# Two-layer MoE behind decayed attention: the first 256 queries' chain leads, score blocks share a bank, the decay's tiles lie on the output buffers

## The chip, the cores and the metric

One core of one Trainium2 chip. The number is the device time of one execution in microseconds (us). TensorE (PE) multiplies matrices from SBUF into PSUM, VectorE (DVE) and ScalarE (ACT) work on both memories, GpSimd (POOL) on SBUF alone, and SyncE (SP) issues nearly all DMAs.

## What is computed

```python
scores = scale * q @ k.T + (cum[:, None] - cum[None, :])      # cum = cumsum(log(clip(f)))
scores = where(causal, scores, -1e9); attn = softmax(scores); x = attn @ v
x = x.reshape(2304, 512)                                      # 4 batches, 8 heads, 576 tokens, 64 a head
h = relu(x @ w_in);  x = (s * h * h + b) @ w_out              # 512 -> 2048 -> 512
h = x @ w_in2;       y = (relu(h) + alpha * min(h, 0)) @ w_out2
```

All inputs are float32, and the result is wanted at that precision: MoE products are made of three passes over values split into a high and a low part.

## The kernel before

All work is written as tasks with an engine (or a choice of engines), a priority from the table `PLAN` and the buffers that they use. A list scheduler in the kernel file runs over them when the program is built and writes the instructions of each engine in the order in which it starts them; on the chip each engine keeps this order and waits on semaphores. Where the scheduler finds PE with nothing to do in the first 50 us of its own reckoning, it puts in a filler (line 482): a matmul of `unit` into the bank `h`, which nobody reads.

The attention of batch 0 is cut into units. Units 0 to 3 are the *pair units*: two heads each and only the first 256 queries, so that blocks 128x128 (chunk 0) and 128x256 (chunk 1) arise for each head. Units 4 to 11 are single heads with the rest of batch 0's queries (128x384, 128x512, and a block for the last 64 rows), later units whole heads of batches 1 to 3. For each block: `t_mm` (line 879, a float32 matmul for batch 0) fills a bank of the ring `s` (three banks), `t_max` (line 887, DVE) adds the mask, writes the block to an `e` tile and takes the row maximum, `t_exp` (892, ACT) takes the exponential and the row sum, `t_eps` (895) and `t_rec` (902) make the reciprocal for a group of blocks, `t_norm` (909, POOL) scales, PE transposes (954), ACT copies to `pt` (963, 965), PE multiplies with `v` (1007), and the output is split into `x` (1013, 1018). A MoE step is line 1057 into `h`, the ReLU (1067, ACT), 1070 to 1080, and line 1089 into `a`.

The decay enters the scores as extra rows of the operands `lk` and `lkx`. For the pair units they are made on chip: `ct` is the running sum of log f (clamp 674, Ln 675, scan 676), copied to the query side (771), multiplied by a column of the selector `sel` on the key side (775), beside a copy of the selector (768, POOL) and ones (765). For other units they go through DRAM: `c8_d` (float32 rows) and, from unit 16 on, `aug_d` (split rows, lines 682 to 689). `ft`, `c8`, `ct`, `aug` and `sel` lie in the pool `fpool`; `to_p1` closes it and opens the pools of `x`, of the MoE buffers and of the outputs `o` in its place, so the first write to `x` (line 1013) waits until the last reader of `fpool` is done.

The weights (`raw`) are loaded as 64-bit words, scaled (520, ACT), put together with three DVE operations (511, 514, 517) and split (534 ACT, 537 POOL).

Of the kernel before, what the change touches and what calls it, by code (L numbers as in the profile page):

```python
# [8 lines left out]
F32 = mybir.dt.float32  # L9
# [41 lines left out]
    t0=-1.0888,  # L51
    ta=0.01,
    tb=9.6508,
    t1=8.6867,
    t2=16.6003,
    t3=15.3984,
    prep=7.7877,
    prepA=43.6581,
    nf=16,
    cp=22.985,  # L60
    ip=-109.7403,
    vp=-33.3287,
    mq=14.5484,
    grp=2,
    grpA=2,
    max=4.2471,
    pv=5.3929,
    f2=-46.0421,
    ap=-14.4232,
    cd=-144.6316,  # L70
    ek=0,
    rw=29.7964,
    ne=20,
    ev='a',
    xh='va',
    gh='va',
    kl='v',
    nr='p',
    cv=(-73.4345, 20.6093, 18.0342, -19.5027, 151.3319, 1.1636, 65.9701, 48.7936, 48.5269, 0.3075, 62.2567, -7.3405, -47.8266, 117.9491, -31.4032, 18.9361),
    blocks=((-14.544, 1.6623), (1.2546, 1.1614), (0.0818, 2.1196), (2.4326, 2.1883), (1.847, 2.8553), (2.9159, 3.0)),  # L80
# [264 lines left out]
def decay_attention_two_moe(ctx: ExitStack, tc: tile.TileContext, qk, qka, v, f, wi1, wo1, wi2, wo2,  # L345
# [39 lines left out]
    def rdma(dst, src):  # L385
# [10 lines left out]
    open_pool("fpool", side="left")  # L396
# [36 lines left out]
        "pt": ring("att", "pt", 2, [P, PTW], F32),  # L433
        "s": ring("psa", "s", 3, [P, 512], F32),
# [7 lines left out]
        "o": ring("p1", "o", 6, [P, 2 * T], F32),  # L442
# [51 lines left out]
    def unpack(key, fc, prio, cv, after=(), view=None, raw=None, at=0.0):  # L494
# [33 lines left out]
    def convert(key, fc, prio, after=()):  # L528
# [9 lines left out]
        task(("act", ac(512, False), t_hi), r=[(K, "v")], w=[(K, "hi")], bufs=[cv, w], prio=prio)  # L538
# [92 lines left out]
    fpool = pools["fpool"][0]  # L631
    LO, HI, BOTH = slice(64, 96), slice(96, 128), slice(64, 128)
    ft = fpool.tile([P, S], F32, name="ft")
    c8_t = fpool.tile([P, 2, 2, S], F32, name="c8")
    c8 = c8_t[LO]
    sel = fpool.tile([P, 2, NHEAD], F32, name="sel")
    one_t = c8_t[BOTH, 0, 1, :]
    ct_t = fpool.tile([P, S], F32, name="ct")
    ct = ct_t[LO]
    aug = fpool.tile([P, 2, 4, S], F32R, name="aug")[LO]  # L640
    augf = aug.bitcast(F32)

# [3 lines left out]
    AUG = [[(k, i) for k in ("chi", "clo", "nchi", "nclo")] + [("aug1", 0), ("aug1", 1)] for i in range(2)]  # L646
# [9 lines left out]
    startup(("sp", 200, lambda: load(ft[LO], f)), w=["f0"])  # L656
    st.append(task(("ad", 200, lambda: aload(ft[HI], f)), w=["f1"], prio=-103.0))
    startup(("dve", 60, lambda: nc.vector.memset(warm, 1.0)), w=["warm"])
    startup(("act", 1400, lambda: nc.scalar.activation(warm, warm, AF.Ln)), r=["warm"], w=["warm"])
    for k, part in (("selA", LO), ("selB", HI)):  # L660
        startup(("sp", 200, lambda part=part: load(sel[part], sel_in)), w=[k])
    startup(("dve", 540, lambda: nc.vector.memset(one_t, 1.0)), w=["one"])
    st.append(task([("dve", 540, lambda: nc.vector.memset(c8[:, 1, 0, :], 1.0)), ("pool", 530, lambda: nc.gpsimd.memset(c8[:, 1, 0, :], 1.0))], w=["one8"], prio=PLAN["ap"]))
    for a in range(2):
        st.append(task(("pool", 1020, lambda a=a: nc.gpsimd.memset(augf[:, a, 1 - a::2, :], 1.0)), w=[("aug1", a)], prio=PLAN["ap"]))
    startup(("pool", 250, const_sums), w=["constsums"])
    for i, (a, z) in enumerate(FPARTS):
        def part(i=i, a=a, z=z, pr=-100.0 if i == 0 else PLAN["f2"]):
            n, fs, cs = z - a, ft[BOTH, a:z], ct[:, a:z]
# [47 lines left out]
    def add_unit(heads, chunks, t0, t1):  # L717
# [13 lines left out]
        units.append(u)  # L731
        return u

    tm = PLAN["t0"]
    for p in range(NPAIR):
        add_unit([2 * p, 2 * p + 1], [0, 1], tm, tm + PLAN["ta"])
        tm += PLAN["ta"]
# [13 lines left out]
    def prep_f32(u):  # L751
# [12 lines left out]
        def t_one():  # L764
            nc.gpsimd.memset(flat(u)[HI, 0, 0:w], 1.0)
# [896 lines left out]
```

## Time and profile before

| | |
|---|---|
| median of 3 runs | 961.25 us (960.94 to 962.83) |
| profiled execution, its own time | 958.43 us |
| its span, first to last instruction | 956.6 us |
| PE busy / DVE / ACT / POOL | 940.1 / 721.9 / 606.4 / 384.8 us |
| mean granted clock of PE | 0.996 of full speed |

Line 482 counts as PE being busy. "Granted clock" 1.00 is 2.4 GHz, 0.50 is 1.2 GHz. A float32 matmul shows as two records in the trace, so "x8" in a row of such matmuls are four. The end of a matmul's record overlaps the next one; the start times are the better measure of the pace.

### The profile page before, as it was taken

To read this page: it belongs to the slowest core of one execution; us is meant where nothing else is said; L and a number is where in the kernel's file an instruction comes from. 1 tells how busy PE (TensorE), PEld (TensorE's weight loads), DVE (VectorE), ACT (ScalarE), POOL (GpSimd) and SP (SyncE) were. 2 spreads that over 40 slices of the span, in tenths; PEclk is the share of its full clock that TensorE was granted. 3 is DMA by queue.
4 is the path that set the end of the run, shared out by engine and by line. 5 is a ranking of instruction groups with operands and counts; after the bars stand their busy time and mean duration, and the time that the engine had idled before them with its cause. 6 is when DMAs were issued, how large, how long until landed. Compare 5 with 4: busy or idle time off the path is not lost.

```text
span 956.6 us, 18667 instructions
## 1 busy us (share of the span) xinstructions
PE 940.1 (98%) x6382; PEld 848.9 (89%) x6382; DVE 721.9 (75%) x1543; ACT 606.4 (63%) x1455; POOL 384.8 (40%) x425
## 2 busy tenths in 40 slices
PE   7899999999999999999999999999999999999998
PEld 6567798899798988988888888899999999999997
DVE  7688877775877656668796896679986869868686
ACT  5688767564767567798676776565654456544552
POOL 5465653451644104478576744124251422513000
PEclk9999999999999999999999999999999999999999
DMA  7674433531544385596869665995698955889566
GB/s 185 190 217 154 159 119 113 174 125 56 174 135 143 101 309 160 154 303 229 319 220 357 237 218 191 338 340 193 186 314 258 319 177 176 252 252 319 164 188 203
DMA packets 99119, 201.44 MB, mean 211 GB/s; under 512 B 10816, under 2 KB 25504, under 8 KB 98352
## 3 DMA queue, kind: packets, MB, share of 16 engines
q1 hardware_dynamic: 98688, 199.78, 64.5%
q8 instruction: 51, 0.84, 0.4%
q10 hardware_dynamic: 336, 0.47, 0.2%
q14 instruction: 44, 0.36, 0.1%
HBM read 146.75 MB, written 50.51 MB: 206 GB/s over the span
## 4 chain that ended last, share of the span: by engine, by line
PE 92%; DVE 5%; DMA 1%; ACT 1%; issue 0%; POOL 0%; SPq 0%; DVEq 0%
PE b L1328 16%; PE h L1057 15%; PE a L1089 9%; PE b L1092 9%; PE a L1390 8%; PE k L1057 6%; PE k L1390 5%; PE h L1390 5%; PE t L1007 5%; PE t L954 4%; PE s L879 4%; PE a L1092 2%; PE s L874 2%; PE s L875 2%; DVE gq L1315 1%; DVE gq L1268 1%
## 5 line engine op out<-in xcount | busy, mean ns | idle before, releaser
L1328 PE MATMUL b<-wp,gj 128*128 128x256 f32 x1368 | 172.4, 278 | 0.8 <-DVE gj L1315 0.7
L1328 PEld LDWEIGHTS b<-wp,gj 128*128 128x128 f32 x1368 | 169.4, 188 | 1.2 <-DVE gj L1315 1.0
L909 POOL TENSOR_SCALAR e<-e,rec 128x128 f32<-128x128 f32 (+4 forms) x144 | 94.1, 665 | 148.0 <-DVE rec L902 45.5
L1057 PE MATMUL h<-x,i 128*128 128x256 f32 (+1 forms) x864 | 146.4, 318 | 0.0
L1057 PEld LDWEIGHTS h<-x,i 128*128 128x128 f32 x864 | 123.9, 188 | 13.6 <-issue 1.2
L1315 DVE TENSOR_TENSOR gj<-gq,gj 128x384 fp32r<-128x384 f32 x152 | 98.9, 660 | 31.6 <-ACT gj L1313 31.0
L1313 ACT CAST gj<-gq 128x384 fp32r<-128x384 f32 x142 | 73.0, 515 | 68.6 <-PE b L1328 64.9
L1268 POOL TENSOR_TENSOR gq<-gq 128x384 f32<-128x384 f32 x33 | 40.0, 1214 | 161.7 <-DVE gq L1430 141.1
L1089 PE MATMUL a<-g,o 128*128 128x256 f32 x768 | 101.4, 281 | 0.0
L1089 PEld LDWEIGHTS a<-g,o 128*128 128x128 f32 x768 | 94.7, 188 | 2.1 <-issue 0.5
L892 ACT ACTIVATE e<-e,ngm 128x128 f32<-128x128 f32 (+4 forms) x144 | 84.1, 586 | 16.0 <-DVE ngm L887 13.8
L1092 PE MATMUL b<-g,o 128*128 128x512 f32 x384 | 93.4, 389 | 0.0
L1092 PEld LDWEIGHTS b<-g,o 128*128 128x128 f32 x384 | 71.8, 188 | 14.5
L887 DVE CUSTOM_DVE_ANT_0 e<-s,mask 128x128 f32<-128x128 f32 (+4 forms) x144 | 67.1, 480 | 20.4 <-PE s L875 8.9
L1111 POOL TENSOR_TENSOR g<-r,g 128x512 fp32r<-128x512 f32 (+1 forms) x42 | 53.5, 1278 | 67.5 <-ACT g L1108 66.2
L1067 ACT ACTIVATE r<-h 128x256 f32<-128x256 f32 (+1 forms) x76 | 34.0, 448 | 52.1 <-PE h L1057 49.9
L954 PE MATMUL t<-ident,e 128*128 128x128 f32 (+1 forms) x400 | 63.9, 275 | 2.7 <-ACT pt L965 1.5
L965 ACT COPY pt<-t 128x256 f32<-128x256 f32 (+2 forms) x128 | 54.3, 451 | 15.0 <-PE t L954 14.6
L1390 PE MATMUL h<-x,wq 128*128 128x384 f32 x288 | 57.6, 335 | 0.0
L511 DVE TENSOR_SCALAR cv<-raw 128x512 int32<-128x512 int32 x48 | 27.6, 576 | 38.2 <-ACT raw L520 33.2
L954 PEld LDWEIGHTS t<-ident,e 128*128 128x128 f32 (+1 forms) x400 | 46.3, 140 | 9.7 <-issue 2.7
L1007 PE MATMUL t<-pt,v 128*64 128x320 f32 (+4 forms) x448 | 52.2, 366 | 0.1
(177 smaller groups left out, 2005.9 us busy)
## 6 DMA issues: line engine op xcount, KB each, us to landing
wp<-w2o_d SPq DMA_DIRECT2D x168, 256.0 KB
wq<-w2i_d SPq DMA_DIRECT2D x112, 256.0 KB
raw<-in_wi_dram SPq DMA_DIRECT2D x29, 512.0 KB
w2o_d<-wq SPq DMA_DIRECT2D x56, 256.0 KB
w2i_d<-wq SPq DMA_DIRECT2D x56, 256.0 KB
raw<-in_wo_dram SPq DMA_DIRECT2D x27, 512.0 KB
rawqk<-in_qk_dram SPq DMA_DIRECT2D x20, 576.0 KB
v<-in_v_dram SPq DMA_DIRECT2D x20, 320.0 KB
```

The source lines that it names most:

```text
L887: nc.vector.tensor_tensor_reduce(e.t[0:rows, k0:k1], st_.t[0:rows, 0:w], mask[0:rows, m0:m0 + w], -0.125 if u.f32 else -1.0, init, ALU.add ...
L892: nc.scalar.activation(x, x, AF.Exp, bias=ng[0:rows, col:col + 1], scale=-1.0, accum_out=sm[0:rows, col:col + 1])
L909: eng.tensor_scalar(x, x, rc[0:rows, col:col + 1], 1.0, ALU.mult, ALU.mult)
L954: nc.tensor.transpose(pp.t[0:kw, i * P:i * P + P], e.t[:, P * kb:P * kb + kw], ident)
L1007: nc.tensor.matmul(o.t[64 * j:64 * j + 64, a - q0:z - q0], vb.t[0:kr, kb, j, :], uu.pt[jj].t[0:kr, kb * PTS + a:kb * PTS + z], start=(i == ...
L1057: nc.tensor.matmul(ps.t[:, 0:w], wv[:, wl, kc, :], x.t[:, kc, xl, x0:x0 + w], start=(n == 0), stop=(n == 3 * KC - 1))
L1089: nc.tensor.matmul(acc[u // 2].t[:, T * (u % 2):T * (u % 2) + T], wo.t[:, wl, u * P:u * P + P], g.t[:, gl, g0:g0 + w], start=(first and i ...
L1092: nc.tensor.matmul(acc[u].t[:, 0:w], wo.t[:, wl, u * P:u * P + P], g.t[:, gl, 0:w], start=(first and i == 0), stop=end)
L1313: task([("act", ac(TH, False), lambda g=g, qv=qv: nc.scalar.copy(g.t[:, 0, :], qv())), ("dvp", dv2(TH), lambda g=g, qv=qv: nc.vector.tenso ...
L1315: task(("dvp", dv(TH), lambda g=g, qv=qv: nc.vector.tensor_tensor(g.t[:, 1, :], qv(), g.t[:, 0, :].bitcast(F32), ALU.subtract)), r=[("G", ...
L1328: nc.tensor.matmul(y[t // 2].t[:, T * (t % 2):T * (t % 2) + T], g.t[:, gl, t * P:t * P + P], wop[k].t[:, wl, :], start=(fresh and k == 0 a ...
L1390: nc.tensor.matmul(b.t[:, 0:TH], wb.t[:, wl, k * P:k * P + P], x[:, k, xl, :], start=(start and m == 0), stop=(m == 5), skip_group_check=True)
```

## The change

The units keep their work. What changes:

- The pair units' priorities (`tA`) now lie ahead of everything else, and the tasks of the startup are ordered for them: both scans directly behind each other, with a broadcast column of ones; all eight `t_q`/`t_k` products before the first maximum; the rows of `c8` on POOL or DVE, `f` loaded before the identity.
- The query side is now the running sum times the selector's column (`t_q`), and the key side's counterpart are ones (`t_one` for both sides), so the copy of the selector on POOL is gone.
- Both blocks of a head go into one bank (`s0`), one `e` tile and one transpose bank; one copy of 384 columns (`transposes_two`) takes them to `pt` or the new ring `pa`. The value product of the pair units goes to the ring `a`. Reciprocals are taken for groups of four blocks (`grp`, `grpA`), normalization may go to POOL or ACT (`nr='pa'`), copies of `pt` to DVE or ACT (`ev='va'`).
- `fpool` is gone. `ct`, `c8` and half of `aug` lie in a tile `F` in the place of the six output buffers `o`, the other half of `aug` in the place of `xs`; `x` has memory of its own from the start.
- All numbers of `PLAN` are new.

```diff
 PLAN = dict(
-    t0=-1.0888,
+    t0=11.8757,
-    grp=2,
-    grpA=2,
+    grp=4,
+    grpA=4,
-    ev='a',
+    ev='va',
-    nr='p',
+    nr='pa',
+    tA=-90.0,
...
-    open_pool("fpool", side="left")
+    open_pool("p1", side="left")
+    open_pool("x0", side="left")
+    open_pool("x1", side="left")
...
+    FW = 72 + 6 * 2 * T
+    F = [pools["p1"][0].tile([P, FW], F32, tag="F", bufs=1, name="F_0")]
+    aug0 = pools["p1"][0].tile([P, 2048], F32R, tag="xs", bufs=1, name="aug0")
+
+    def o_at(n):
+        return F[1][:, 72 + 2 * T * (n % 6):72 + 2 * T * (n % 6) + 2 * T]
...
-        "o": ring("p1", "o", 6, [P, 2 * T], F32),
+        "o": Ring(6, o_at),
...
+    ct_t, big = F[0][:, 0:S], F[0][:, S:S + 8 * (S - QA)]
+    c8 = big[LO, 0:4 * S].rearrange("p (a r s) -> p a r s", a=2, r=2)
+    aug = [x[HI].rearrange("p (a r s) -> p a r s", a=2, r=4) for x in (aug0, big.bitcast(F32R))]
...
-        def t_one():
-            nc.gpsimd.memset(flat(u)[HI, 0, 0:w], 1.0)
-
-        def t_sel():
-            nc.gpsimd.tensor_copy(both(1, LO), sel[LO, 0, n:n + 2].unsqueeze(2).to_broadcast([32, 2, QA]))
-
-        def t_q(copy):
-            copy(both(0, LO), ct_t[LO, 0:QA].unsqueeze(1).to_broadcast([32, 2, QA]))
+        def t_one(eng, side):
+            eng.memset(flat(u)[(HI, LO)[side], side, 0:w], 1.0)
+
+        def t_q(eng):
+            for j in range(2):
+                dst, k = flat(u)[LO, 0, QA * j:QA * j + QA], sel[LO, 0, n + j:n + j + 1]
+                if eng is nc.scalar:
+                    eng.activation(dst, ct_t[LO, 0:QA], AF.Copy, scale=k)
+                else:
+                    eng.tensor_scalar(dst, ct_t[LO, 0:QA], k, None, ALU.mult)
...
-            ps = [R["s"].buf() for _ in parts]
-            e = u.e[j, c] = R[f"e{c + 2 * j if u.two else c}"].buf()
+            s0 = P * c if u.two else 0
+            if u.two and c == 1:
+                e = u.e[j, c] = u.e[j, 0]
+            else:
+                ps = [R["s"].buf() for _ in parts]
+                e = u.e[j, c] = R[f"e{2 + (2 * U + j) % 3 if u.two else c}"].buf()
...
+    def transposes_two(u):
+        U = u.i
+        for j in range(2):
+            u.pt[j] = R["pt" if U % 2 else "pa"].buf()
+            pp, x = R["t"].buf(), u.pt[j]
...
+            def t_ev(copy, x=x, pp=pp):
+                copy(x.t[:, 0:3 * P], pp.t[:, 0:3 * P])
...
     def to_p1():
-        close_pool("fpool")
-        open_pool("p1", side="left", reuse_waits="tile")
...
+        F.append(pools["p1"][0].tile([P, FW], F32, tag="F", bufs=1, name="F_1"))
```

How this moves instructions. In the rows below a line number is that of the kernel they come from (879 before is 906 after, 887 is 914, 775 is 800, 1013 is 1062); numbers behind a name are buffers; in square brackets are the semaphores waited for, DMAHW being a load. On DVE, from the second scan (`ct` or `F`) to the first row maximum (ISA with `mask`), before:

```order
L676 SCALAR_TENSOR_TENSOR ct<-c_132,ct,ft 64x320 [waits Activation_49]
L775 TENSOR_SCALAR lkx_155<-ct,sel 32x256 x2
L511 TENSOR_SCALAR cv_242<-raw_170 128x512 [waits DMAHW6_49,Activation_49]
L682 CAST aug<-ct 32x256
L514 SCALAR_TENSOR_TENSOR cv_242<-raw_170,cv_242 128x512 [waits DVE_49]
L683 TENSOR_TENSOR aug<-ct,aug 32x256 [waits DVE_49]
L517 SCALAR_TENSOR_TENSOR cv_242<-raw_170,cv_242 128x512 [waits DVE_49]
L689 TENSOR_SCALAR aug<-aug 32x256 [waits DVE_49]
L682 CAST aug<-ct 32x320
L775 TENSOR_SCALAR lk_161<-ct,sel 32x256 x2
L683 TENSOR_TENSOR aug<-ct,aug 32x320 [waits DVE_49]
L887 ISA e_0_292,ngm_126<-s_221,mask 128x128 [waits DMAHW7_49,PE_49]
```

and after, from the first scan on:

```order
L697 SCALAR_TENSOR_TENSOR F_94<-ones,F_94 64x256 [waits Activation_49]
L697 SCALAR_TENSOR_TENSOR F_94<-ones,F_94 64x320 [waits DVE_49,Activation_49]
L796 TENSOR_SCALAR lkx_147<-F_94,sel 32x256 [waits DMAHW3_49]
L796 TENSOR_SCALAR lkx_147<-F_94,sel 32x256
L800 TENSOR_SCALAR lkx_147<-F_94,sel 32x256 [waits DMAHW4_49]
L800 TENSOR_SCALAR lkx_147<-F_94,sel 32x256
L800 TENSOR_SCALAR lkx_155<-F_94,sel 32x256 x2
L800 TENSOR_SCALAR lkx_162<-F_94,sel 32x256 x2
L800 TENSOR_SCALAR lk_169<-F_94,sel 32x256 x2
L914 ISA e_0_270,ngm_139<-s_246,mask 128x128 [waits DMAHW6_49,PE_49]
L914 ISA ngm_139 128x1
L914 ISA e_0_270,ngm_139<-s_246,mask 128x256
```

The weight conversion (`cv`) and the split of the decay (`aug`) no longer stand ahead of the first maximum; the eight scalings of the key side (800) and the two of the first unit's query side (796) follow the scans directly.

On PE, the first score blocks behind the first run of fillers, before:

```order
L879 MATMUL s_221<-lkx_140 128x128 [waits DMAHW3_49,DVE_49,Pool_49]
L879 MATMUL s_225<-lkx_140 128x256
L879 MATMUL s_229<-lkx_140 128x128 [waits DVE_49]
L482 LDWEIGHTS unit
L482 MATMUL h_142<-unit 128x256
```

and after:

```order
L906 MATMUL s_246<-lkx_147 128x128 [waits DMAHW2_49,DVE_49,Pool_49]
L906 MATMUL s_246<-lkx_147 128x256
L906 MATMUL s_254<-lkx_147 128x128 [waits DVE_49]
L906 MATMUL s_254<-lkx_147 128x256
L906 MATMUL s_258<-lkx_155 128x128 [waits DVE_49,DMAHW5_49,Activation_49,Pool_49]
L906 MATMUL s_258<-lkx_155 128x256
L500 LDWEIGHTS unit
L500 MATMUL h_149<-unit 128x256
```

Six blocks in three buffers of the ring (s_246, s_254 and s_258) stand ahead of the next filler, where three blocks in three buffers stood.

On DVE, the first writing of `x` and what stands around it, before (DMAHW2 is the store of `aug` to `aug_d`):

```order
L902 RECIPROCAL rec_125<-sums_123 128x2 [waits Activation_49]
L887 ISA e_2_401,ngm_126<-s_366,mask 128x256 [waits DVE_49,PE_49,Pool_49]
L887 ISA ngm_126 128x1
L902 RECIPROCAL rec_124<-sums_122 128x2 [waits DVE_49,Activation_49]
L1013 CAST x_444<-t_413 128x256 [waits DMAHW2_49,PE_49]
L511 TENSOR_SCALAR cv_452<-raw_297 128x512 [waits Activation_49]
```

and after:

```order
L1062 CAST x_401<-a_379 128x256 [waits PE_49]
L929 RECIPROCAL rec_137<-sums_135 128x4 [waits Activation_49]
L1067 TENSOR_TENSOR x_401<-a_379,x_401 128x256 [waits DVE_49]
L980 COPY pt_392<-t_391 128x384 [waits PE_49]
L980 COPY pt_397<-t_396 128x384 [waits PE_49]
```

The cast to `x` waits for PE alone now; copies of 384 columns from the transposes' banks follow it. On PE as a whole, 134 fillers became 94, of which 45 stand ahead of the first score (38 before); the last 2749 matmuls are in the same order.

## Rows read from the trace of the kernel before

**Rows 1.** The page, part 1: busy us (share of span) x instructions.
```profile
PE 940.1 (98%) x6382; PEld 848.9 (89%) x6382; DVE 721.9 (75%) x1543; ACT 606.4 (63%) x1455; POOL 384.8 (40%) x425
```

**Rows 2.** Groups by line, 0 to 48 us: count | busy us, mean ns.
```profile
L482 PE MATMUL h<-unit 128*128 128x256 bf16 x134 | 22.6, 312 | 0.9 <-POOL sums L654 0.9
```

**Rows 3.** The chain that ended last, 0 to 60 us: start us, us, what.
```profile
24.23 4.71 DMA aug_d<-aug
...
40.28 1.12 PE s L879 x8
...
43.20 1.51 PE s L879 x4
44.70 0.80 PE t L1007 x8
...
47.56 0.44 PE t L954 x4
47.99 1.42 PE h L1057 x12
```

**Rows 4.** PE timeline: start, us, line, operation [idle before <- releaser].
```profile
0.88 7.18 PE L482 MATMUL h<-unit 128*128 128x256 bf16 x38 [0.88 <-POOL sums L654]
...
9.43 3.86 PE L482 MATMUL h<-unit 128*128 128x256 bf16 x33
16.92 1.22 PE L879 MATMUL s<-lkx 128*128 128x256 f32 x2 [3.63 <-DVE ngm L887]
...
30.12 0.78 PE L879 MATMUL s<-lk 128*128 128x256 f32 x2 [2.69 <-DVE ngm L887]
```

**Rows 5.** Two microseconds: length, busy us per engine, PEclk (granted clock), DMA.
```profile
18.00:20.00 2.00, 2.00 (x9) 1.57 (x8) 0.85 (x5) 1.86 (x10) 0.00 (x0) 0.50 0.28 71
```

**Rows 6.** DVE's timeline, 0 to 50 us, columns as in rows 4.
```profile
3.58 1.70 DVE L674 TENSOR_SCALAR ft<-ft 64x256 f32<-64x256 f32 x2 [1.41 <-DMA ft<-in_f_dram]
5.21 1.10 DVE L676 TENSOR_TENSOR_SCAN ct<-c,ft 64x256 f32<-64x256 f32 x1
...
9.40 0.88 DVE L676 TENSOR_TENSOR_SCAN ct<-c,ct,ft 64x320 f32<-64x320 f32 x1
10.32 0.82 DVE L775 TENSOR_SCALAR lkx<-ct,sel 32x256 f32<-32x256 f32 x2
...
14.39 1.63 DVE L775 TENSOR_SCALAR lk<-ct,sel 32x256 f32<-32x256 f32 x2
...
16.56 0.29 DVE L887 CUSTOM_DVE_ANT_0 e<-s,mask 128x128 f32<-128x128 f32 x1
...
29.04 0.42 DVE L1013 CAST x<-t 128x256 fp32r<-128x256 f32 x1 [3.98 <-DMA aug_d<-aug]
```

**Rows 7.** POOL's timeline, 0 to 50 us.
```profile
0.96 1.44 POOL L765 MEMSET lkx<- 32x512 f32 x3
...
2.90 2.20 POOL L665 MEMSET aug<- 32x1152 f32 x2
...
14.61 1.26 POOL L537 TENSOR_TENSOR i<-cv,i 128x512 fp32r<-128x512 f32 x1 [3.62 <-ACT i L534]
```

**Rows 8.** ACT's timeline, 0 to 50 us.
```profile
23.52 0.39 ACT L892 ACTIVATE e<-e,ngm 128x128 f32<-128x128 f32 x1
...
23.91 0.49 ACT L892 ACTIVATE e<-e,ngm 128x256 f32<-128x256 f32 x1
```

**Rows 9.** From the first ReLU to the eighth, columns as in rows 5.
```profile
49.40:107.80 58.40, 57.87 (x400) 42.34 (x399) 49.33 (x131) 47.99 (x143) 33.69 (x38) 1.00 0.61 192
```

**Rows 10.** Groups of ACT there: count | busy, mean ns | idle before, releasers.
```profile
L892 ACT ACTIVATE e<-e,ngm 128x512 f32<-128x512 f32 (+4 forms) x25 | 15.9, 638 | 2.3 <-DVE ngm L887 2.3
L965 ACT COPY pt<-t 128x256 f32<-128x256 f32 (+2 forms) x27 | 11.8, 467 | 2.3 <-PE t L954 2.3
L520 ACT ACTIVATE raw<-raw 128x512 f32<-128x512 f32 x11 | 7.7, 697 | 1.1 <-DMA raw<-in_wi_dram 0.7 <-DMA raw<-in_wo_dram 0.4
...
L1074 ACT ACTIVATE g<-r,small 128x256 fp32r<-128x256 f32 x6 | 3.0, 508 | 0.1
```

More of the change, by code (lines that the diff above doesn't have):

```diff
@@ L628, in outs_of @@
             task(("sp", kb_of(P * 2048), lambda i=i: rdma(w2t_d[p // CH][i][:, p % CH], st_.t[:, i])), r=done, w=[("w2t", p, f"t{i + 1}")], bufs=[st_], prio=prio)
-    fpool = pools["fpool"][0]
     LO, HI, BOTH = slice(64, 96), slice(96, 128), slice(64, 128)
[L633 to L641, printed above, removed]
+    ct_t, big = F[0][:, 0:S], F[0][:, S:S + 8 * (S - QA)]
+    c8 = big[LO, 0:4 * S].rearrange("p (a r s) -> p a r s", a=2, r=2)
+    sel = pools["att"][0].tile([P, 2, NHEAD], F32, name="sel")
+    ones = pools["att"][0].tile([P, 1], F32, name="ones")
+    aug = [x[HI].rearrange("p (a r s) -> p a r s", a=2, r=4) for x in (aug0, big.bitcast(F32R))]
+    augf = [x.bitcast(F32) for x in aug]
+    ft = ct_t
     HF32 = max(H, PLAN["nf"] - H // 2)
     FPARTS = ((0, QA), (QA, S))
-    AUG = [[(k, i) for k in ("chi", "clo", "nchi", "nclo")] + [("aug1", 0), ("aug1", 1)] for i in range(2)]
+    AUG = [[(k, i) for k in ("chi", "clo", "nchi", "nclo")] + [("aug1", 0, i), ("aug1", 1, i)] for i in range(2)]
     st = []
@@ L732, in add_unit @@
         return u
[L734 removed]
+    tm = PLAN["tA"]
     for p in range(NPAIR):
@@ L828, in prep @@
         task(("sp", kb_of(P * 8 * w), t_load), r=["attr"], w=[(U, "raw")], bufs=[u.raw], prio=pr)
-        task(("sp", 100 if not u.two else 700, t_rows), r=["augd"], w=[(U, "rows")], bufs=[u.lk], prio=pr)
+        task(("sp", 100 if not u.two else 700, t_rows), r=[("augd", 0), ("augd", 1)], w=[(U, "rows")], bufs=[u.lk], prio=pr)
         task(("pool", pl1(w) - 80, t_khi), r=[(U, "raw")], w=[(U, "khi"), (U, "klo")], bufs=[u.raw, u.ka], prio=pr)
@@ L917, in scores @@
                 if uu.two:
-                    need += [(uu.i, k) for k in ("raw", "one", "sel", "q", "k")]
+                    need += [(uu.i, "raw"), (uu.i, "one", 0), (uu.i, "one", 1), (uu.i, "q"), (uu.i, "k")]
                 elif uu.f32:
@@ L999, in products, with t_pv @@
             xs = {blk: xbuf(blk) for blk, *_ in pieces}
-            o = R["t"].buf()
+            o = R["a" if u.i < PLAN["pa"] else "t"].buf()
             K = (u.i, "o", part)
-            def t_pv(part=part, q0=q0, seq=seq, o=o):
+            def t_pv(part=part, q0=q0, seq=seq, o=o, step=P if u.two else PTS):
                 for i, (kb, a, z) in enumerate(seq):
@@ L1099, in moe_step @@
                      w=[(K, "h")] + ([("open", name, fc)] if kc == 0 else []), bufs=[ps, x, wi], prio=pr1)
-        PG = ["pg2"] if big else ["p1"]
+        PG = ["pg2"] if big else []
         def g_hi():
```

150 lines of the change are left out of this document (85 added, 65 removed).

## The prediction

> **What bounds the kernel now.** The page first: TensorE (PE) is busy for 940.1 of 956.6 us [rows 1], so the time is the sum of what PE has to do plus whatever keeps it from useful work. But a part of that busy time is not work: line 482 issues filler matmuls into a bank nobody reads, 134 of them, all before 48 us [rows 2]. So I read the start next, in the chain of waits and in PE's timeline, and ask how much of the first 47.56 us was useful. 47.56 is where the last filler ends; from there the chain is solid PE work [rows 3].
>
> Useful by then, priced from [rows 3]: the float32 scores of 384 and 512 columns take 1.51 us, 1.69 ns a column, so the 16 score blocks of the first 256 queries (8 heads of 128+256 columns) are 5.2 us; three pairs of 384+512 blocks 4.5; the block of the last 64 rows 1.12; 27 transposes at 0.11 are 3.0; four value products at 0.80 are 3.2. Together 17.0 us. **Dead time is 47.56 - 17.0 = 30.5 us.** It has three faces. PE stood still for 3.63 us before 16.92 and for 2.69 before 30.12 [rows 4]. After the first stand the granted clock was 0.50, that is 1.2 GHz instead of 2.4, for more than 2 us [rows 5], and a similar stretch followed the second. The rest is fillers.
>
> Why it stood shows in VectorE's (DVE) timeline [rows 6]. The first row maximum (16.56) stands behind the selector products, the decay's split and a weight conversion, and until it has read a score bank PE has no fourth bank. And at 29.04 DVE had idled 3.98 us for the store of aug to DRAM (24.23 to 28.94 in [rows 3]): x, which it wants to write, lies on the memory of aug.
>
> **The change, part by part.** The program's tail is untouched: the last 2749 matmuls, 374 ScalarE (ACT), 544 DVE and 84 GpSimd (POOL) instructions stand in the same order. Useful PE work is the same; fillers go from 134 to 94. So I count dead time anew, up to the last filler of the new order.
>
> *Ahead of the first score* stand 45 fillers instead of 38. The 38 ended at 8.06, and 33 dense ones took 3.86 us, 0.117 each [rows 4]: 8.06 + 7 x 0.117 = 8.9. Is the data there? DVE now begins with four memsets of 32x512 (0.48 each on POOL, [rows 7]), so to about 3.2, where the clamps stood at 3.58 before; then the clamps, Ln on ACT and the two scans, 1.10 and 0.88 [rows 6]: clamps 3.3 to 3.9, first scan 4.5 to 5.6, second to 6.4. The scans read a broadcast column of ones instead of a 64x576 tile; no row shows the form, and I price it as before. Then ten scalings of 32x256. [rows 6] show 0.41 (two in 0.82) and 0.82 (two in 1.63, while POOL ran the two-input subtraction of 14.61 in [rows 7]). I take 0.41, because POOL has one-input work at this place, scalings and memsets. Four make the first unit's operands: 8.05, before PE comes. All ten end at 10.5; by 0.82 at 14.6. Up to 0.5 each they cost PE nothing, by the next paragraph. POOL's selector copies go; ACT scales the other three units' queries meanwhile, six from about 6.5 on, each 0.4 to 0.5 like the exponentials of 128 and 256 columns [rows 8], hidden behind fillers and the first unit's scores.
>
> *Two blocks in one bank.* Three banks now hold six blocks instead of three, so PE runs six before it needs a maximum read. The first maximum of a pair waits for both matmuls: at most the 256-column one, 0.43 us. It costs nothing, as the first three banks are full at 8.9 + 2.0 = 10.9 and DVE comes at 10.5 anyway and is then the slower: 0.29 for 128 columns [rows 6] and at most 0.58 for 256, against PE's 0.65 a pair. PE's eight fillers behind the sixth block last to 11.8. The Trainium skill (PSUM — Partial Sum Buffer, section on bank collisions) speaks against such sharing: no two engines may be in one bank at once. By it each pair is written whole, then read whole, as this order does; the sum stays as it is. With eight evictions less (one of 384 columns for 128 and 256) ACT and DVE save some 1.5 us, used up below.
>
> *The overlay.* x no longer lies on aug: the wait of 3.98 us is gone, with PE's 2.69. The aug store, now in two pieces, still takes about 4.7 us of the queues, and SP issues it ahead of the next two weight loads; what is late next is the scaling of those weights on ACT, at about 30 us.
>
> *The walk.* First maximum 10.5, first exponential 10.9; a pair of exponentials is 0.39 + 0.49 (starts in [rows 8]). Reciprocals now serve four blocks and stand behind twelve maxima: 14.5. POOL and ACT normalize from 14.7, the first transposes are possible at 15.6, when PE has done its 16 scores (8.9 + 0.9 of fillers + 5.2 = 15.0) and five more fillers. From there PE's fillers and ACT run level: ACT's list (16 exponentials 7.0, 6 norms 2.5, reciprocal sums, one eviction and one weight scaling) fills 10.9 to about 22, when PE is at the second value product. I find waits of 0.5 us in all. Useful work up to the last filler is 5.2 + 2.6 + 3.2 + 1.5 + 1.12 + 0.65 = 14.3; the 49 later fillers at 0.11 are 5.4. **Last filler at 8.9 + 5.4 + 14.3 + 0.5 = 29.1, dead time 14.8.** The first MoE step, 5.6 us of work later, ends at 34.8; it ended at 49.41 [rows 3]. **Gain up to here: 30.5 - 14.8 = 15.7 us**, of which 6.3 are the two stands, some 5 the low clock and 4.3 fillers.
>
> *What is given back.* Between the first and the eighth ReLU PE was full before: 57.87 of 58.40 us, ACT at 47.99 [rows 9]. The new order puts more attention in this stretch: 8 score matmuls, 13 transposes and 14 value products more, about 6.8 us, so PE wants 65.2. ACT has 8 more exponentials (0.64 each), 22 norms that POOL used to do, 2 more weight scalings (0.70) and a gate (0.51), 7 evictions less (0.4) [rows 10]. No ACT norm is in the trace; between the gate's 0.51 for 256 columns and the scaling's 0.70 for 512, less their overlap, I take 0.5 (0.4 to 0.7: 8.8 to 15.4). That is 48.0 + 5.1 + 11.0 + 1.4 + 0.5 - 2.8 = 63.2. ACT also waited 3.4 us there for others than PE: 2.3 for maxima, 1.1 for weight loads [rows 10]. 63.2 + 3.4 = 66.6 against 65.2: ACT is the bound by 1.4, and its waits grow when DVE gets some of its evictions. I take 4.5 us, between 0 (ACT ahead) and 12.
>
> **Sum.** 15.7 - 4.5 = 11.2 us off the profiled execution: span 945.4, time 958.43 - 11.2 = 947.2. The three runs' median is 961.25, 2.8 above the profiled execution; the same 11.2 off it gives **950.0 us**.
>
> **Rivals.**
> *A, nothing is given back*: ACT runs ahead of PE, norms nearer 0.4. For it: 0.53 us of PE idleness in that stretch before [rows 9]. Against: ACT at 97% of PE's need. 961.25 - 15.7 = 945.5.
> *B, ACT becomes the bound of the first blocks*: norms at 0.7 and waits doubled make 67.6 + 6.8 = 74.4, nine over PE's 65.2; 954 to 959.
> *C, the start is slow again*: each of the ten scalings waits for POOL, 0.82 us, all done at 14.6. PE has six blocks done and its eight fillers out at 11.8, and stands until 15: as long as the 3.63 us before, and with the half clock after it (some 2 us), 5.5 us lost: 955.5. For it: the 1.63 row, and the clamps, two in 1.70 beside POOL's memset of 2.90 [rows 6, 7]. Against: the scalings of 0.41. The Trainium skill (SBUF — State Buffer, SBUF: two separate sides) has a rule for it: VectorE's two-port modes and GpSimd lock a shared port pair for a whole instruction, and the loser blocks. The two rows agree. By that rule each scaling waits for up to one POOL instruction, which is C.
> *D, slower*: ACT's queue stalls for so long that the head start is spent. Counted by columns as above, the eighth ReLU stands behind 78.0 us of useful work in the new order and 70.4 in the old; at PE's pace of the stretch (58.4 us for 52.5) PE had done as much at about 107.8 + 8.4 = 116 before. The new kernel is slower if ACT gets there later: 34.9 + 63.2 leaves 18 us for waits. The place would be the weight scalings behind the aug store, and the norms behind reciprocals of four blocks. With 22 us it ends at 965. Against: 10.4 us of idleness in all before, most of it for PE.
> *E, the overlay is one tile for six outputs* and could make them wait for each other. The order of the tail shows the same waits as before; under 0.01.
>
> **How the numbers follow.** Forecast (947 to 953) 0.57, A 0.13, B 0.16, C 0.07, D 0.07. The order after 108 us changes too, up to the common tail; of PE's 16.5 us of idleness [rows 1] some 9 lie behind 48 us, and for a sixth of them each end carries 1.5 more. The range 943 to 958 (A less 1.5 and one for the bounds of the scalings and norms; B nearly to its end) leaves out D and little else. 0.2% is 1.9 us, about what a measurement of this kernel can tell from no change: faster 0.88, the same 0.05 (the end of B), slower 0.07.
>
> **What would show it.** 94 fillers, the last ending near 29; no stretch with granted clock 0.50 after the first score; DVE's first maximum near 10.5 and no idle for the aug store ahead of x; the first MoE step ending near 34.8, the eighth ReLU near 104.5; PE idle there of a few us, released by ACT. A first maximum at 14 or later is C, an eighth ReLU past 110 B, past 116 D.

## The result: 951.8 us, a little over the forecast

The changed kernel takes **951.77 us** (median of 4 runs, 950.27 to 952.06) against 961.1 for the kernel before beside it: ratio 0.9897, 95% interval 0.988 to 0.9915. Forecast were 950.0, range 943 to 958, faster with 0.88. Its profiled execution took 952.06 us, with a span of 950.3; that of the kernel before had taken 958.43, 6.4 more.

The page of the changed kernel (engine totals) and its group of fillers, which answer to [rows 1] and [rows 2]:

```profile
PE 934.7 (98%) x6342; PEld 842.7 (89%) x6342; DVE 722.4 (76%) x1558; ACT 622.7 (66%) x1458; POOL 324.2 (34%) x342
...
L500 PE MATMUL h<-unit 128*128 128x256 bf16 x94 | 14.8, 306 | 0.9 <-POOL unit L439 0.9
```

PE's timeline of the changed kernel (columns as in [rows 4]), from the first filler to the end of the first blocks:

```profile
0.88 7.26 PE L500 MATMUL h<-unit 128*128 128x256 bf16 x45 [0.88 <-POOL unit L439]
7.98 2.13 PE L906 MATMUL s<-lkx 128*128 128x128 f32 x12
9.95 1.06 PE L500 MATMUL h<-unit 128*128 128x256 bf16 x8
12.63 2.21 PE L906 MATMUL s<-lkx 128*128 128x128 f32 x12 [1.63 <-DVE ngm L914]
...
30.42 0.51 PE L500 MATMUL h<-unit 128*128 128x256 bf16 x3
37.28 0.91 PE L906 MATMUL s<-lkx 66*128 66x384 f32 x2 [0.52 <-DVE ngm L914]
39.55 0.98 PE L1003 MATMUL t<-ident,e 128*128 128x128 f32 x7 [0.81 <-ACT pt L1014]
...
92.76 0.33 PE L1003 MATMUL t<-ident,e 128*128 128x128 f32 x1 [2.63 <-ACT pt L1014]
```

The two stands of [rows 4], 3.63 and 2.69 us, are gone; one of 1.63 is left, for the first row maximum ("x12" in the rows around it are six score blocks). The last filler ends at 30.93 (47.56 before) and the first ReLU, right behind the first MoE step, starts at 36.79 (49.55 before). Then PE stands again at three places where it hardly did before: 0.52, 0.81 and 2.63 us. DVE's timeline shows why the first maximum, at 11.84, is late:

```profile
3.17 0.53 DVE L695 TENSOR_SCALAR F<-F 64x256 f32<-64x256 f32 x2
4.45 1.67 DVE L697 TENSOR_TENSOR_SCAN F<-ones,F 64x256 f32<-64x256 f32 x2 [0.75 <-ACT F L696]
6.04 0.83 DVE L796 TENSOR_SCALAR lkx<-F,sel 32x256 f32<-32x256 f32 x2
6.91 3.56 DVE L800 TENSOR_SCALAR lkx<-F,sel 32x256 f32<-32x256 f32 x6
10.39 1.42 DVE L800 TENSOR_SCALAR lk<-F,sel 32x256 f32<-32x256 f32 x2
11.84 0.29 DVE L914 CUSTOM_DVE_ANT_0 e<-s,mask 128x128 f32<-128x128 f32 x1
...
19.88 0.43 DVE L1062 CAST x<-a 128x256 fp32r<-128x256 f32 x1
```

The ten scalings take 0.41 (two), 0.59 (six) and 0.71 us (two) each. And the first x, at 19.88, waits for nothing: the 3.98 us behind the store of aug in [rows 6] are gone.

**The clock.** A second record of the same kernel (c_after below) has the same stand of 2.63 us, and yet the granted clock (last but two) differs behind it. Two microseconds at 94, first of the profiled execution of the result, then of that second one, and its stand:

```profile
94.00:96.00 2.00, 2.00 (x12) 1.67 (x12) 1.73 (x7) 1.76 (x7) 0.71 (x1) 0.50 0.25 100
```

```profile
94.00:96.00 2.00, 2.00 (x18) 1.30 (x16) 1.98 (x7) 2.00 (x8) 0.73 (x1) 1.00 0.25 102
```

```profile
92.79 0.33 PE L1003 MATMUL t<-ident,e 128*128 128x128 f32 x1 [2.63 <-ACT pt L1014]
```

The half clock (0.50, that is 1.2 GHz) lasts about 3.5 us and costs half of that; the spans are 950.3 and 948.4. Every run lists its mean granted clock, so an estimate of the loss can be taken out of each: (1 - clock) times the span. The clock is listed to 0.001, so one such value is good to some 0.5 us. The kernel before had 0.992 to 0.997 in the 39 runs that list it, its profiled execution 0.996, so 958.43 - 0.004 x 956.6 = 954.6 at the full clock; those 39 runs come to 954.4 in the mean, and to 954.2, 954.3 and 954.5 on the three chips that ran them. The changed kernel had 0.998 in six of eight runs and 1.000 in two, and those two took 950.27 and 950.22. **So about 4.4 of the 9.3 us between the medians are waits and fillers, and some 5 are a clock that falls less often.** Only the second part moves with the runs: the kernel before had medians of 958.2, 960.0 and 959.9 beside the experiments. Why its clock falls more often is not shown beyond the stands of [rows 4] that are gone.

### The profile page after: what moved, and what is told of

The parts are those of the page before. It is cut to its first block, busy times and chain, and to the rows that moved or that the text cites. A ratio compares the mean times of both kernels' runs of the same rounds, so it can differ in the third digit from the quotient of the medians.

```text
span 950.3 us, 18342 instructions
## 1 busy us (share of the span) xinstructions
PE 934.7 (98%) x6342; PEld 842.7 (89%) x6342; DVE 722.4 (76%) x1558; ACT 622.7 (66%) x1458; POOL 324.2 (34%) x342
## 3 DMA queue, kind: packets, MB, share of 16 engines
q1 hardware_dynamic: 99184, 199.78, 65.2%
## 4 chain that ended last, share of the span: by engine, by line
PE 93%; DVE 4%; ACT 2%; issue 1%; DVEq 0%
PE b L1377 17%; PE h L1106 14%; PE b L1141 9%; PE a L1138 9%; PE a L1439 8%; PE k L1106 6%; PE k L1439 5%; PE h L1439 5%; PE t L1056 5%; PE t L1003 4%; PE s L906 3%; PE a L1141 2%; PE s L901 2%; PE s L902 2%; ACT pt L1014 1%
## 5 line engine op out<-in xcount | busy, mean ns | idle before, releaser
L1141 PEld LDWEIGHTS b<-g,o 128*128 128x128 f32 x384 | 71.8, 188 | 14.6
L936 POOL TENSOR_SCALAR e<-e,rec 128x256 f32<-128x256 f32 (+4 forms) x66 | 42.0, 646 | 105.2 <-DVE rec L927 42.5
L1160 POOL TENSOR_TENSOR g<-r,g 128x512 fp32r<-128x512 f32 (+1 forms) x34 | 45.1, 1329 | 75.5 <-ACT g L1157 71.0
L1003 PE MATMUL t<-ident,e 128*128 128x128 f32 (+1 forms) x376 | 59.3, 277 | 6.2 <-ACT pt L1014 4.2
L1003 PEld LDWEIGHTS t<-ident,e 128*128 128x128 f32 (+1 forms) x376 | 43.6, 140 | 16.6 <-ACT pt L1014 5.7
L1439 PEld LDWEIGHTS h<-x,wq 128*128 128x128 f32 x288 | 49.4, 188 | 0.2
L1056 PE MATMUL t<-pt,v 128*64 128x320 f32 (+3 forms) x416 | 48.3, 368 | 0.2 <-ACT pt L1014 0.2
L1056 PEld LDWEIGHTS t<-pt,v 128*64 128x64 f32 (+1 forms) x416 | 26.0, 135 | 23.6 <-issue 5.1
```

The costliest lines, as they stand in the source:

```text
L1003: nc.tensor.transpose(pp.t[0:kw, i * P:i * P + P], e.t[:, P * kb:P * kb + kw], ident)
L1056: nc.tensor.matmul(o.t[64 * j:64 * j + 64, a - q0:z - q0], vb.t[0:kr, kb, j, :], uu.pt[jj].t[0:kr, kb * step + a:kb * step + z], start=(i ...
L1141: nc.tensor.matmul(acc[u].t[:, 0:w], wo.t[:, wl, u * P:u * P + P], g.t[:, gl, 0:w], start=(first and i == 0), stop=end)
L1160: eng.tensor_tensor(g.t[:, 1, g0:g0 + w], r_of(), g_hi().bitcast(F32), ALU.subtract)
L1439: nc.tensor.matmul(b.t[:, 0:TH], wb.t[:, wl, k * P:k * P + P], x[:, k, xl, :], start=(start and m == 0), stop=(m == 5), skip_group_check=True)
```

## The experiments

Each time is the median of the runs of that kernel; "at 0.998" names the mean granted clock, and "at the full clock, estimated" the mean of the runs less (1 - clock) times the span; for the changed kernel that is 950.1. Most edits that change a task make the planner arrange the whole list anew; where an edit was put in behind the planner, the text says "in the same order".

**c_after: once more, unchanged.** 

> The changed kernel once more, unchanged, as the measure for the other runs beside it. Its ratio to the kernel before was 0.9897 (0.988 to 0.9915); the same is expected here, whatever the level of this chip.

951.84 (950.22 to 952.06), ratio 0.9919 (0.9898 to 0.994). The level of the changed kernel is the same on both occasions; that of the kernel before moves with its clock.

**e1_norms16: ScalarE's normalizations cut to 16 columns, in the same order.**

```
+ if U >= 2 * NPAIR // 2 and U < NPAIR + 2 * H:      # NPAIR <= U
+     x = x[:, 0:16]
  nc.scalar.activation(x, x, AF.Copy, scale=rc[0:rows, col:col + 1])
```

> The changed kernel with the same order of instructions, but ScalarE's normalizations of the units 4 to 19 (one head with all or most of its queries each) scale 16 columns only; the rest of those blocks stays unnormalized. Theory 1 (ACT's work is the bound of the first blocks): ACT is relieved of some 22 x 0.4 = 9 us between the first and the eighth ReLU, PE's idle time there (3.96 us in the changed kernel) falls under 1 us, the stretch of half clock behind the stand at 90 us is gone, and the time is 945 to 948. Rival (PE stood there for banks or weights, not for ACT's load): idle time stays above 3 us and the time within 1 us of the changed kernel's 951.8.

950.35 (949.6 to 952.99). From the first to the eighth ReLU, the stretch of [rows 9], first of c_after, then of this kernel (both at 1.000):

```profile
37.00:106.40 69.40, 65.66 (x453) 47.14 (x454) 58.83 (x169) 63.24 (x174) 29.25 (x27) 1.00 0.60 190
```

```profile
36.80:105.70 68.90, 65.71 (x454) 47.23 (x454) 59.23 (x169) 56.87 (x174) 29.39 (x27) 1.00 0.60 191
```

ACT loses 6.4 us of work and the stretch 0.5; the span goes from 948.4 to 947.8. PE's idle time there is 3.19 us (3.74 in c_after), and the stand at 90 us shrinks from 2.63 to 1.90, as the four normalizations ahead of it in ACT's list are shorter:

```profile
92.07 0.33 PE L1005 MATMUL t<-ident,e 128*128 128x128 f32 x1 [1.90 <-ACT pt L1016]
```

Theory 1 falls: ACT's amount of work is not what bounds these blocks.

**e2_noeps: without the 24 additions of 1e-9, in the same order.**

```
  def t_eps(c0=cols[0], c1=cols[-1] + 1):
-     nc.scalar.activation(sm[:, c0:c1], sm[:, c0:c1], AF.Copy, bias=1e-9)
+     pass
```

> The changed kernel in the same order without the 24 ScalarE instructions that add 1e-9 to the row sums (a sum is at least 1, so float32 keeps it as it is). Each takes 0.2 us alone and about 0.1 between two others. Theory 1 (ACT is the bound between 37 and 108 us): some 1 to 2 us of ACT's work go there, and reciprocals come 0.1 to 0.3 earlier; time 949.5 to 951, PE idle in that stretch 2 to 3.5 us. Rival (ACT's queue is not what PE waits for): 951 to 952.5.

951.73 (950.09 to 953.57); 950.09 at 1.000 against 950.22 for c_after: no difference, which again speaks against ACT as the bound. Its profile shows the half clock at another place, behind the small stands at 37 and 39 us:

```profile
41.00:45.00 4.00, 4.00 (x11) 1.31 (x12) 0.88 (x3) 3.37 (x8) 0.42 (x2) 0.50 0.42 133
```

**e6_evict: the two evictions that PE waits for at 90 us go to VectorE, all else in the same order.**

```
+ if t.idx == 133:                 # last step of a conversion: behind them
+     self.kept = fn
+ elif t.idx in (552, 553):        # the two evictions
+     [o[2] for o in t.opts if o[0] == "dve"][0]()
```

> The changed kernel in the same order but for two evictions of transposes (128x256 each), for which PE stood from 90.14 to 92.76: VectorE does them instead of ScalarE, ahead of the last step of a weight conversion. Theory (PE stood because these evictions are late in ScalarE's list, behind a ReLU, a gate and four normalizations, not because ScalarE has too much to do): the stand shrinks from 2.63 to about 1 us, the half clock behind it is shorter or gone, and the time is 1.5 to 3 us below the changed kernel beside it. Rival (ScalarE or VectorE as a whole is behind): PE stands as long a little later, time within 0.7 us.

The place first. The chain of waits of the changed kernel from 88 us on:

```profile
88.21 0.59 ACT pt L1014
88.80 0.52 ACT o L555
89.31 0.70 ACT e L934 x2
90.01 0.27 ACT r L1116
90.28 1.11 ACT e L934 x2
91.40 0.40 ACT g L1123
91.80 0.39 ACT e L919 x2
92.18 0.54 ACT pt L1014 x2
92.72 0.04 issue
92.76 0.33 PE t L1003
```

PE's transposes of 89.4 fill both t banks. Their evictions stand in ACT's list behind a weight conversion, four normalizations, a ReLU, its gate and an exponential. In e6_evict PE stands 1.47 us:

```profile
91.64 0.30 PE L1010 MATMUL t<-ident,e 128*128 128x128 f32 x1 [1.47 <-DVE pt L1021]
```

Of the theory, the place is shown. The median is not lower: 952.49 (950.97 to 954.49). At 0.998 it takes 950.97 and 950.99, 0.9 less than c_after at 0.998, but two of its four runs had a clock of 0.994 and 0.995. At the full clock, estimated, the four come to 949.0, 1 us below the changed kernel, where 1.5 to 3 were expected. And the shorter stand did not keep the clock up; it was at 0.50 from about 93 to 96:

```profile
94.00:96.00 2.00, 2.00 (x11) 1.67 (x12) 1.27 (x5) 1.27 (x5) 0.20 (x1) 0.50 0.51 193
```

**e4_quiet and e5_held: GpSimd quiet while VectorE scales.** e4_quiet plans GpSimd's work later (`t.at = 16e3`, everything planned anew). e5_held keeps the order and makes GpSimd wait:

```
+ # ahead of GpSimd's scalings by 8 and memsets, behind VectorE's last k scaling
+ nc.gpsimd.tensor_copy(al_t[HI, 0:1], flat(u)[HI, 1, 2 * QA - 1:2 * QA])
```

> The changed kernel with GpSimd's six memsets for the decay's tiles and the scalings by 8 planned for 16 us instead of 7.5 (the list is planned anew), so that GpSimd is quiet while VectorE scales. Theory (the scalings of 0.59 and 0.71 us waited for GpSimd): each takes about 0.41, first maximum near 10.4 instead of 11.84. Rival (the form itself takes 0.59): durations unchanged, first maximum 11.5 to 12. The time is not the question: the decay's rows come later and it needs more fillers; 950 to 956.

> The changed kernel in the same order; GpSimd's scalings by 8 and memsets, all but the first of them, now wait for VectorE's last k scaling (a copy of one column of its result to GpSimd stands ahead of them). Theory (the scalings of 0.59 and 0.71 us waited for GpSimd): ten scalings at about 0.28 to 0.41, first maximum at 9.3 to 10.4 instead of 11.84, first exponential 2 us earlier, PE's stand before 12.63 gone, last filler 1.5 to 2.5 us earlier, time 1.5 to 2.5 us below the changed kernel beside it. Rival 1 (what GpSimd does comes 4 us later, and the weights' loads behind the store of the decay's rows in SP's queue with it): last filler no earlier, time the same or up to 2 us above. Rival 2 (the gain is given back in the first blocks): last filler and first MoE step earlier, time the same.

e4_quiet: the six scalings take 0.28 each, first maximum 9.24; 958.14 (953.9 at the full clock, estimated), as the list came out otherwise. e5_held, DVE's timeline and then two rows of PE's:

```profile
6.76 1.70 DVE L808 TENSOR_SCALAR lkx<-F,sel 32x256 f32<-32x256 f32 x6
8.38 0.61 DVE L808 TENSOR_SCALAR lk<-F,sel 32x256 f32<-32x256 f32 x2
9.03 0.29 DVE L924 CUSTOM_DVE_ANT_0 e<-s,mask 128x128 f32<-128x128 f32 x1
```

```profile
15.86 0.66 PE L986 MATMUL t<-ident,e 128*128 128x128 f32 x4 [0.83 <-POOL e L946]
...
29.65 0.51 PE L508 MATMUL h<-unit 128*128 128x256 bf16 x3
```

The scalings fall from 0.59 and 0.71 to 0.28 and 0.31, so they did wait for GpSimd. The first maximum comes 2.8 us earlier, but the last filler only 0.8: PE goes through eight fillers that stand behind the sixth score block in any case, and GpSimd, now late itself, holds up the first transposes by 0.83. The time is 950.8 (949.57 to 952.45); at 1.000 949.57 against 950.22. The theory had 1.5 to 2.5 both for the last filler and for the time: right on the scalings, wrong on what they are worth.

**e3_firstmax: the first maxima ahead of the other pairs' scalings, planned anew.**

```
- st.append(task(("dve", 2 * 390, t_k), r=[("c", 0), "selB"], w=[(U, "k")], bufs=[u.lk], prio=pr))
+ st.append(task(("dve", 2 * 390, t_k), r=[("c", 0), "selB"], w=[(U, "k")], bufs=[u.lk], prio=pr + 5 * U))
```

> The changed kernel with VectorE's k scalings of the second to fourth pair of heads put behind the first pair's two maxima (5 x the pair's number on their priority; the list is planned anew with it). First maximum near 9.5 instead of 11.84, first exponential near 9.9 instead of 12.24. Theory 1 (ACT's chain, started by the first maximum, sets the walk to the last filler and the first blocks): last filler about 2 us earlier, time 949 to 950.5. Rival 1 (PE then waits for the scalings of the later pairs, which end near 13 to 14): the stand only moves, time within 1 us of 951.8. Rival 2 (the head start is given back to ACT in the first blocks): last filler earlier, first MoE step earlier, time the same.

962.35 (961.93 to 963.65): 10.5 slower than the changed kernel, 9.6 at the full clock, estimated. The first maximum and PE's longest stand:

```profile
10.29 0.29 DVE L914 CUSTOM_DVE_ANT_0 e<-s,mask 128x128 f32<-128x128 f32 x1
...
38.22 1.23 PE L906 MATMUL s<-lkx 66*64 66x288 f32 x4 [2.35 <-DVE ngm L914]
```

The first ReLU is at 32.13, 4.7 earlier. Everything won is lost later, and more: PE stands 2.35 us at 38 and in smaller pieces over the whole span (PE busy 941.8 of 961.9). This is more than rival 2 had allowed.

**e9_orderonly: the kernel before with the first 256 queries leading, and nothing else.**

```
- tm = PLAN["t0"]          # pairs of heads of the first 256 queries
+ tm = -90.0               # 0.1091 apart; the other units from 11.8757 on
```

> The kernel before with one part of the change: the four pairs of heads of the first 256 queries get the changed kernel's place in the list (-90, 0.1091 apart; the other units' from 11.8757 on), planned anew with all other numbers as before; one score block a bank, the overlay and the selector copies stay. Theory (the head start is worth only what the rest of the list keeps, and x still waits for the store of aug): first maximum 12 to 15, first MoE step 40 to 47, time 953 to 960. Rival 1 (leading with the first 256 queries is the whole gain): 950 to 953. Rival 2 (it is a loss without the other parts): above 961.

970.97 (969.89 to 971.44): rival 2. DVE's timeline at x, and its longest wait (us in total, times, longest):

```profile
33.12 0.42 DVE L1014 CAST x<-t 128x256 fp32r<-128x256 f32 x1 [3.99 <-DMA aug_d<-aug]
```

```profile
DVE ft L674 <- DMA ft<-in_f_dram: 9.1, 1, 9.1
```

SP now issues the load of f behind the loads of the four pairs, at 4.7 us (1.2 before), and DVE waits 9.1 us for it. x still waits for the store of aug. The first ReLU comes at 55.15, 5.6 later than before. So the lead alone does not pay in the old list. These two waits, 9.1 and 3.99 us, are what the change's edits of the loads and of the memory of aug remove; that those edits are enough to make the lead pay is not shown, as all other numbers of `PLAN` are the old ones here.

**e10_banks: one score block a bank again, planned anew.**

```
  e = u.e[j, c] = u.e[j, 0]
+ ps = [R["s"].buf() for _ in parts]
```

> The changed kernel with one score block a bank again for the first 256 queries, planned anew with the same numbers. Theory (two blocks in a bank let PE run six blocks ahead of the first maximum): PE has three blocks done when it waits, its stand or fillers ahead of the first maximum (11.8) are about 1 us longer, and the last filler comes 0.5 to 2 us later; with the list planned anew the time may move by several us besides, 951 to 960. Rival (the banks are not what PE waits for): the 16th score block ends within 0.3 us of the changed kernel's.

PE's timeline from the first score block on (two records a block, so "x6" are three blocks):

```profile
7.51 1.04 PE L907 MATMUL s<-lkx 128*128 128x128 f32 x6
8.39 1.39 PE L500 MATMUL h<-unit 128*128 128x256 bf16 x11
12.21 1.44 PE L907 MATMUL s<-lkx 128*128 128x256 f32 x6 [2.42 <-DVE ngm L915]
...
15.70 1.25 PE L907 MATMUL s<-lkx 128*128 128x256 f32 x6
...
20.26 0.60 PE L907 MATMUL s<-lk 128*128 128x256 f32 x2
```

At the first maximum (11.85) PE has three blocks done, where it had six, and stands 2.42 instead of 1.63. The 12th block ends at 16.95 instead of 14.84; the 16th, which in this list stands behind transposes and value products, at 20.86 instead of 16.15. So the rival falls: PE does wait for banks. But the last filler ends at 26.03, 4.9 earlier, where the theory had 0.5 to 2 later (first ReLU 34.42, time 958.23, 956.94 to 961.49). The list is another, so what the shared banks are worth by themselves is not measured.

**e11_nofill: no fillers after 8 us, planned anew.** `FILL = 8e3` instead of `50e3`.

> The changed kernel without its fillers after 8 us (45 of the 94 stay), planned anew. Theory (fillers hold the granted clock up while PE waits for the first blocks' chain): PE stands for 5 to 7 us between 10 and 31, a stretch with granted clock 0.50 follows, last useful work of the walk up to 3 us later; time 952 to 958. Rival (fillers are in PE's way): the walk is 1 to 3 us shorter, time 948 to 951.

Stretches of this kernel (columns as in [rows 5]):

```profile
10.00:14.00 4.00, 1.49 (x9) 1.22 (x9) 3.97 (x18) 1.75 (x8) 2.51 (x5) 1.00 1.03 330
...
18.00:24.00 6.00, 4.98 (x31) 2.83 (x31) 5.47 (x18) 5.88 (x23) 1.64 (x5) 1.00 0.79 219
```

PE stands 2.51 us at once and 4.2 in all, where 5 to 7 were expected, and the granted clock stays at 1.00 to 31 us; the first ReLU is at 35.25, 1.5 earlier. So here the theory fails and the rival holds as far as the walk goes. The time, 959.84 (956.58 to 964.44), is far above the rival's 948 to 951: the mean clock is lower (0.989 to 0.997), which is some 4 of the 8 us above the changed kernel, and the list is another (953.7 at the full clock, estimated).

**e7_augwait: one instruction that should have waited for the store of aug.**

```
+ nc.vector.memset(aug[0][:, 0, 0, 0:1].bitcast(F32), 0.0)   # ahead of the first x
```

> The changed kernel in the same order with one instruction more: VectorE writes one column of the memory of aug ahead of the first x, and so waits for the store of aug to DRAM as x did before the change. The store is issued at 21.1 us, after x is wanted (19.88), so VectorE stands for some 4 us if the store takes as long as before. Theory (that wait on VectorE stops PE, as before): PE stands or runs fillers at the half clock behind it, last filler 2 to 4 us later, time 2.5 to 6 us above the changed kernel beside it. Rival (in the new order other work hides it): time within 1 us.

It waited for nothing: the store stands behind it in the program, so the store waits for it.

```profile
19.81 0.06 DVE L1063 MEMSET aug<- 32x1 f32 x1
19.90 0.42 DVE L1065 CAST x<-a 128x256 fp32r<-128x256 f32 x1
```

951.84, the changed kernel's time. What x's wait would cost in the new order is not measured. The new order writes x 1.2 us before the store of aug is even issued (21.1), which it could not if both lay on one memory.

**e8_best: what e5_held and e6_evict point to, in the same order.** GpSimd waits for the scalings, aug's memsets and negations stand behind its first two normalizations, the eight fillers go, and VectorE does the two evictions.

```
+ if t.idx in (26, 7, 27, 8): self.late.append(fn)              # until the last k scaling
+ elif t.idx in (9, 10, 11, 12, 21, 31): self.later.append(fn)  # until two normalizations are out
...
+ if 8e3 < now < 10.9e3: return True                            # no filler here
```

> The changed kernel in the same order with four edits: GpSimd's scalings and memsets wait for VectorE's last k scaling (as in e5_held); the memsets and negations of aug's tiles stand behind GpSimd's first two normalizations instead of ahead of them; the eight fillers between the sixth and the seventh score block are left out; and the two evictions of e6_evict are VectorE's. From e5_held: first maximum near 9.0; PE goes on at about 10.1 instead of 11.2, so the 16th maximum and the first reciprocal come near 12.9 instead of 13.87, and GpSimd is free for it. Theory (the first maximum's 2.8 us were lost to the eight fillers and to GpSimd's list): last filler 1.5 to 2.5 us earlier than the changed kernel's 30.95, time 948 to 949.5 with the same granted clock as the changed kernel's median (0.998), 946.5 to 948 at 1.000. Rival (the walk is set elsewhere, by PE's later fillers and ACT's exponentials): last filler near 30.1 as in e5_held, time 949.5 to 951.

**948.27 us (948.07 to 948.93)**, ratio 0.9888 (0.9868 to 0.9907): faster than both kernels, 3.5 below the changed one's median, 2.0 where both run at 1.000. PE's timeline:

```profile
9.98 2.21 PE L928 MATMUL s<-lkx 128*128 128x128 f32 x12 [0.40 <-DVE ngm L936]
...
18.51 0.33 PE L998 MATMUL t<-ident,e 128*128 128x128 f32 x1 [1.61 <-POOL e L958]
...
29.18 0.50 PE L520 MATMUL h<-unit 128*128 128x256 bf16 x3
```

The last filler ends at 29.68, 1.25 earlier (1.5 to 2.5 were expected, and 946.5 to 948 for the time at 1.000): the next stand, 1.61 us at 18.51, is for a normalization that GpSimd now does behind the memsets moved there. The first ReLU comes 1.3 earlier than in c_after and the eighth 1.8, so some 0.5 is won in the first blocks, where PE's stand for the two evictions is 1.48. Its clock was 0.999 or 1.000 in all four runs.

## Why the prediction was right, and where its steps were not

**The direction and the larger part.** Dead time at the start, by the same prices as in the prediction, is 30.93 - 14.3 = 16.6 us, where 14.8 was forecast and 30.5 stood before: a gain of 13.9 instead of 15.7. The stands of 3.63 and 2.69 and the half clock behind them are gone, as predicted (priced at some 5 us; by its mean clock of 0.996 the kernel before lost 3.8); there are 94 fillers, and x waits for nothing. One sign failed: the clock was to stay up after the first score, and in the profiled execution it was at 0.50 from 94 to 97. One term erred the other way: the fillers ahead of the first score were out at 8.0, not 8.9, so PE was through its six blocks and eight fillers at 11.0 and stood the longer for the late maximum. How much each part of the change won is not shown: the runs that take back one part (e7_augwait, e9_orderonly, e10_banks) either changed nothing or got another list.

**"I take 0.41, because POOL has one-input work at this place": wrong.** POOL's memsets and scalings slowed the ten scalings to 0.41, 0.59 and 0.71, and the first maximum came at 11.84 instead of 10.5. With GpSimd quiet they take 0.28 to 0.35 (e5_held). That was rival C in part: at 0.82 each it had them end at 14.6, and PE stand 3 us with half clock behind; PE stood 1.63 and the clock held. All of GpSimd's hindrance is worth 2.8 us at the first maximum and, by e5_held, only 0.8 at the last filler. The Trainium skill (SBUF — State Buffer, SBUF: two separate sides) says that VectorE, in its two-port modes, and GpSimd take a shared port pair from each other for a whole instruction; e4_quiet and e5_held agree that VectorE is hindered (0.28 against 0.59). By that rule the two take turns; from 6.9 to 10.3 each starts six instructions in the changed kernel, by turns (VectorE at 7.26, 7.92, 8.38, GpSimd at 7.13, 7.82, 8.26), which fits, but no run here separates turns from a shared width.

**"ACT is the bound by 1.4": wrong, though its numbers held.** At the full clock PE has 65.66 us of work between the first and the eighth ReLU (65.2 forecast) and ACT 63.24 (63.2). But e1_norms16 takes 6.4 us from ACT and wins 0.5. What PE loses there, 69.40 - 65.66 = 3.74 us, is 2.63, 0.81 and 0.3 (what is left of 0.48 at 37) at three places where one eviction or maximum stands late in a queue; the largest is shown by the chain and by e6_evict, the other two are read from the timeline alone. The forecast of "PE idle there of a few us, released by ACT" was right for another reason than the one given. It also follows that rival B, a bound by ACT, has no ground here.

**"I take 4.5": 5.7 were given back, and the clock took 1.9 more.** Span before 956.6, c_after 948.4 at the full clock: 8.2 of the 13.9 remain. PE's additional idle time between 36 and 300 us is 6.9 - 2.9 = 4.0; the other 1.7 is not placed, and the prices by which I counted the work done at the last filler may hold it. Rival A, nothing given back, falls with this. In the profiled execution of the result the half clock at 94 takes 1.9 on top, so 6.4 of the forecast 11.2 are left. The eighth ReLU came at 107.76, and at 106.11 in c_after, where 104.5 was forecast.

**The level: right by two errors.** The prediction added 2.8 us because the median of before was that much above its profiled execution. That distance is before's alone: its clock varies from 0.992 to 0.997, the changed kernel's from 0.998 to 1.000, and the changed kernel's median lies 0.3 below its profiled execution. So 4.8 us too much gain and 3.1 us too much on top nearly cancel, and the forecast is 1.8 off. That it came so close is luck.

**D and E** did not happen: the eighth ReLU stays far from 116, and GpSimd's additions into the output buffers wait as long as before (12.7 us in both traces from 500 us on).

## What to carry to other kernels

A head start is worth what the list behind it keeps: four lists planned anew reached the first ReLU 1.5 to 4.7 us earlier and ended 6 to 11 us later (3.7 to 9.6 at the full clock, estimated), and the lead put into the old list lost 11. Before calling an engine the bound by its sum of work, look at what stands ahead of the one instruction that is waited for: taking 6.4 us of work from ScalarE won 0.5, while e8_best, which takes no work away but eight fillers, won 2.0. Compare runs at the same mean clock, or the clock is taken for the change.

## What was not expected of the hardware

The granted clock does not follow from the program alone. The same stand of 2.63 us in the same kernel was followed by 3.5 us at 0.50 in one execution and by none in another; in e2_noeps the clock fell at about 40, behind stands of 0.52 and 0.81 us that the changed kernel has too, and stayed at 0.50 for nearly 7 us; behind its stand at 94 it did not fall. The stands of 3.63 and 2.69 us of the kernel before were followed by half clock in its trace ([rows 4, 5], and the row below for the second), and so was the one of 1.47 in e6_evict; one of 2.51 at the start of e11_nofill and those of 1.61 and 1.48 in e8_best were not. And a scaling of 32x256 on VectorE takes 0.28 us beside a quiet GpSimd, under half of the 0.59 and 0.71 beside its memsets.

```profile
32.00:34.00 2.00, 2.00 (x5) 1.20 (x4) 0.72 (x4) 1.79 (x8) 0.82 (x2) 0.50 0.60 152
```
